# Table rows of 96 elements instead of 94, and one output store issued from another queue

## The chip, the cores and the metric

The kernel runs on one core of a Trainium2 chip. The metric is device time in microseconds of one execution, as the median of several runs; lower is better. A profile of one more execution shows each engine: TensorE (PE, with its weight loads as PEld), VectorE (DVE), ScalarE (ACT), GpSimd (POOL) and SyncE (SP), which here only issues DMAs.

## What is computed

A global filter along the sequence, then a feed-forward block with an exact GELU:

```python
X = np.fft.rfft(x, axis=1)                     # x: 8 x 3008 x 256
y = np.fft.irfft(X * (filt_r + 1j * filt_i), n=3008, axis=1)
h = y.reshape(24064, 256) @ w_in               # w_in: 256 x 2048
out = (0.5 * h * (1 + erf(h / sqrt(2)))) @ w_out   # w_out: 2048 x 256
```

Inputs and the output are float32.

## The kernel before

The sequence of 3008 is split as 47 x 64, and the Fourier transform and its inverse are each two stages of small matrix products with tables of sines and cosines. Per batch `b` the stages are `s1` (transform over 47), `s2` (over 64, then the product with the filter on VectorE), `s3` (inverse over 64) and `s4` (inverse over 47), with round trips through DRAM (`R1`, `R2`; written and read back by SP) to turn the data between them. Batch 0 has stages of its own (`c1` to `c4`), since nothing else runs beside them.

`s4` is the stage that the change touches. For each of 8 groups `grp` of positions and 2 halves of the channels it issues 4 matmuls (L513), each with 96 x 128 weights out of `d_sb` and, as the moving operand, one row of the table `T4a`: 94 columns, row number `4 * grp + i`. So there are 7 batches x 8 x 2 x 4 = 448 of them, in 112 groups of four; a group fills one PSUM bank, which ScalarE or VectorE copies (L329, L333) into the ring `y_sb`. Batch 0's `c4` (L611) has the same shape of matmul, with one table `T4c` of 96 x 94 for all its positions.

`T4a` is 96 partitions x 32 rows x 94 elements in bf16, the real and imaginary parts of a row interleaved. GpSimd makes it in `table_4_all` in four calls, each with two parts; a part is two products into a scratch tile (L410) and their sum into every second element of eight rows (L412).

The feed-forward block runs in tiles `t` of 512 rows, 47 of them. `mm1` (L635, L638) is the first product and the GELU. `mm2_first` is the second product for tile 0; for the others `mm2_seven` (L707) forms it from seven quarter-size products, as in Strassen's method, of sums that VectorE makes (`sums_1` to `sums_3`; L676, L682, L689), and VectorE combines the seven in L722 to L736 into output tiles `ost`. Each output tile of 512 rows is stored in pieces of 128 rows by `put_rows` (L754), in the order h = 1 then h = 0, and sub = 0 then 1 in each; a piece that crosses a group of 376 rows becomes two DMAs. Tiles 0 and 1 are stored by SP and the later ones by GpSimd.

The order of everything is written out by hand. The main loop at the end of the kernel goes through slots, 16 for a tile: in each slot first come the pieces that a table `at` has put there (stages of the filter for the batch ahead, loads, table work), then a share of `mm2_seven` of the tile before and then `mm1`. Each engine and each DMA queue works through its own instructions in that order. `load_next` puts a tiny copy on GpSimd (`gate`, L149) that waits for VectorE, ahead of loads of the next batch (L98), so that these don't start early. The output buffers `ost` and `t_sb` come from one pool of four.

DMAs of a kind (hardware: issued by SP or ACT; software: issued by GpSimd) take eight completion counters in turn, and a DMA waits for the one that had its counter before it.

Of the kernel before, what the change touches and what calls it, by code (L numbers as in the profile page):

```python
# [12 lines left out]
BF16 = mybir.dt.bfloat16  # L13
# [5 lines left out]
NA, NB = 47, 64  # L19
K1 = 24  # L20
HB = 32
# [10 lines left out]
class _Mix:  # L32
    def __init__(self, ctx, tc, x, filt_r, filt_i, w_in, w_out, out):
        self.tc, self.nc = tc, tc.nc
        self.x, self.filt_r, self.filt_i = x, filt_r, filt_i
        self.w_in, self.w_out, self.out = w_in, w_out, out
        self.B, self.S, self.D = x.shape
        self.DFF = w_in.shape[1]
        assert self.S == NA * NB and self.D == 256 and self.DFF == 2048
        pool = lambda name, bufs, **kw: ctx.enter_context(tc.tile_pool(name=name, bufs=bufs, **kw))  # L40
        P = bass.MemoryType.PSUM
        self.const = pool("const", 1)
        self.px = pool("px", 1)
        self.pa = pool("pa", 3)
        self.pb = pool("pb", 3)
        self.pp = pool("pp", 3)
        self.pv = pool("pv", 2)
        self.pd = pool("pd", 3)
        self.pool = pool
        self.po = pool("po", 4)  # L50
        self.py = pool("py", 1)
        self.pg = pool("pg", 2)
        self.pq = pool("pq", 1)
        self.small = pool("small", 1)
        self.dram = pool("dram", 2, space=bass.MemoryType.DRAM)
        c = self.const
        self.T1 = c.tile([2 * NA, 96], BF16, name="T1")
        self.T2p = c.tile([128, K1, 2, 2, 16], BF16, name="T2p")
        self.xs = c.tile([128, 4, 256], BF16, name="xs")
        self.U = c.tile([128, 2, 2, HB], BF16, name="U")  # L60
        self.T4a = c.tile([96, HB, 2 * NA], BF16, name="T4a")
        self.T4c = c.tile([96, NA, 2], BF16, name="T4c")
        self.F = c.tile([128, 2, K1, 256], BF16, name="F")
        self.w_in_sb = c.tile([128, 2, self.DFF], BF16, name="w_in_sb")
        self.w_out_sb = c.tile([128, 16, self.D], FP16, name="w_out_sb")
        self.w_sums = c.tile([128, 4, 8, 128], FP16, name="w_sums")
        self.ps, self.st = {}, {}
        self.flip = 0
# [333 lines left out]
    def table_4_all(self, parts):  # L402

        tt = self.nc.gpsimd.tensor_tensor
        tmp = self.pd.tile([96, 1024], FP32, tag="d", name="tmp_sb")
        a, b = (tmp[:, o:o + 8 * NA].rearrange("p (w m) -> p w m", w=8) for o in (0, 512))
        to = self.T4a.rearrange("p w (m h) -> p h w m", h=2)
        for w, h in parts:
            for o, x in ((a, 0), (b, 1)):
                tt(out=o, in0=self.fcs[:, w:w + 8, h, x:x + 1].to_broadcast([96, 8, NA]),  # L410
                   in1=self.G[:, x].unsqueeze(1).to_broadcast([96, 8, NA]), op=ALU.mult)
            tt(out=to[:, h, w:w + 8], in0=a, in1=b, op=ALU.add)  # L412
# [94 lines left out]
    def s4(self, b, grp, half, eng):  # L507
        nc = self.nc
        o = b % 2 * self.S
        d = self.st[b, "d", grp // 2]  # L510
        ps = self.bank("ps_s4")
        for i in range(4):
            nc.tensor.matmul(ps[:, 94 * i:94 * i + 94],  # L513
                             lhsT=d[:, (grp % 2) * 4 + i, 128 * half:128 * half + 128],
                             rhs=self.T4a[:, 4 * grp + i], start=True, stop=True)
        if b == self.B - 1:
            yv = self.ring[:, half, o:o + self.S].rearrange("c (m w) -> c m w", w=HB)[:, :, 4 * grp:4 * grp + 4]
        else:
            o += GRP * grp
            yv = self.ring[:, half, o:o + GRP].rearrange("c (m w) -> c m w", w=4)  # L520
        pv = ps[:, 0:376].rearrange("c (i m) -> c m i", i=4)
        self._evac(yv, pv, eng, 1.0 / self.S)
# [168 lines left out]
    def mm2_seven(self, t, lo, hi):  # L691

        nc, v = self.nc, self.nc.vector.tensor_tensor
        a11, a12, s2, a22 = self.quarters(t)
        w = self.w_out_sb.rearrange("p (i k) (n o) -> p k n i o", k=2, n=2)
        q = self.w_sums
        s31, s4 = self.st["s", t], self.st.get(("s4", t))
        ops = ((a11, w[:, 0, 0]), (a12, w[:, 1, 0]), (s2, q[:, 1]), (s31[:, :, 0], q[:, 2]),
               (s31[:, :, 1], q[:, 0]), (a22, q[:, 3]), (s4, w[:, 1, 1]))
        last = t == self.B * self.S // TCH - 1  # L700
        for n in range(lo, hi):
            m, sub, i = n // 16, n // 8 % 2, n % 8
            if n % 16 == 0 and (m == 0 or m % 2 == 1) or last and m > 4 and i == 0:
                self.st["o"] = self.bank("ps_o", "h" if n > 80 else "o").rearrange("p (m s o) -> p m s o", m=2, s=2)
            ps = self.st["o"]
            a, b = ops[m]
            nc.tensor.matmul(ps[:, (m + 1) % 2, sub, :], lhsT=a[:, i, 128 * sub:128 * sub + 128], rhs=b[:, i],  # L707
                             start=i == 0, stop=i == 7)
            if last and m > 4 and i == 7:
                self.finish(t, m, sub, ps)  # L710
            if n % 16 != 15 or m % 2 or last and m > 4:
                continue
            p0, p1 = ps[:, 0], ps[:, 1]
            if m == 0:
                self.st["t"] = self.po.tile([128, 2, 2, 128], FP32, tag="ost", name="t_sb")
                self.st["c"] = [None, None]
            if m in (2, 4):
                self.st["c"][m // 4] = self.po.tile([128, 2, 256], FP32, tag="ost", name="ost")
            t1, t3 = self.st["t"][:, 0], self.st["t"][:, 1]
            c = lambda h, k: self.st["c"][h][:, :, 128 * k:128 * k + 128]  # L720
            if m == 0:
                nc.vector.tensor_copy(out=t1, in_=p1)  # L722
            elif m == 2:
                v(out=c(0, 0), in0=t1, in1=p0, op=ALU.add)  # L724
                if last:
                    self.store(t, 0, 0, nc.sync)
                v(out=t1, in0=t1, in1=p1, op=ALU.add)
            elif m == 4:
                v(out=t3, in0=t1, in1=p0, op=ALU.subtract)  # L729
                v(out=c(1, 1), in0=t3, in1=p1, op=ALU.add)  # L730
                if last:
                    self.store(t, 1, 1, nc.scalar)
                v(out=t1, in0=t1, in1=p1, op=ALU.add)
            else:
                for h, tt, p in ((1, t3, p0), (0, t1, p1)):
                    v(out=c(h, 1 - h), in0=tt, in1=p, op=ALU.add)  # L736
                    for sub in range(2):
                        self.put_rows(t * TCH + 256 * h + 128 * sub, self.st["c"][h][:, sub],
                                      nc.gpsimd if t > 1 else nc.sync)

    def put_rows(self, r0, tile_, eng):

# [282 lines left out]
```

## Time and profile before

| | us |
|---|---|
| runs before | 743.26, 743.35, 744.1; median 743.35 |
| span of the profiled execution, first to last instruction | 741.6 |
| TensorE busy | 731.2 |
| VectorE busy | 584.7 |
| ScalarE busy | 574.6 |
| GpSimd busy | 292.9 |
| L513, 448 matmuls: busy, mean of one | 38.1, 0.206 |
| L412, 8 sums on GpSimd: busy, mean of one | 10.7, 1.336 |
| L410, 16 products on GpSimd: busy, mean of one | 14.1, 0.902 |
| L754, 227 store issues on GpSimd: busy, mean of one | 128.8, 0.574 |

The profiled execution has its own time: between its span and the median of the runs lie 1.75 us, in which no instruction of the page runs. Matmuls are pipelined, so that the lengths of neighbours overlap; the distance from one start to the next is what a matmul costs. PE's busy share therefore says that work was there, not that the array was at its peak. DMA issues count as busy time on POOL only.

### The profile page before, as it was taken

To read this page: it belongs to the slowest core of one execution; us is meant where nothing else is said; L and a number is where in the kernel's file an instruction comes from. 1 tells how busy PE (TensorE), PEld (TensorE's weight loads), DVE (VectorE), ACT (ScalarE), POOL (GpSimd) and SP (SyncE) were. 2 spreads that over 40 slices of the span, in tenths; PEclk is the share of its full clock that TensorE was granted. 3 is DMA by queue.
4 is the path that set the end of the run, shared out by engine and by line. 5 is a ranking of instruction groups with operands and counts; after the bars stand their busy time and mean duration, and the time that the engine had idled before them with its cause. 6 is when DMAs were issued, how large, how long until landed. Compare 5 with 4: busy or idle time off the path is not lost.

```text
span 741.6 us, 20996 instructions
## 1 busy us (share of the span) xinstructions
PE 731.2 (99%) x8588; PEld 507.9 (68%) x8588; DVE 584.7 (79%) x1036; ACT 574.6 (77%) x1048; POOL 292.9 (39%) x546
## 2 busy tenths in 40 slices
PE   7999999999999999999999999999999999999997
PEld 4856665666776666666777666666677666777776
DVE  7986988889877897788976889678888887675666
ACT  6997778678877888777887778877888778777773
POOL 7995356674313452135511364115531212121121
PEclk9999999999999999999999999999999999999999
DMA  9999643646265643645626555255545443311011
GB/s 150 224 201 233 163 110 97 194 102 140 76 156 143 133 101 98 188 100 125 133 85 171 120 116 137 74 156 141 110 100 136 137 111 106 92 45 43 31 58 58
DMA packets 84051, 90.79 MB, mean 122 GB/s; under 512 B 13347, under 2 KB 63011, under 8 KB 83827
## 3 DMA queue, kind: packets, MB, share of 16 engines
q1 hardware_dynamic: 61011, 49.11, 25.8%
q0 software_dynamic: 22528, 40.15, 24.3%
q8 instruction: 67, 1.10, 0.6%
q14 instruction: 29, 0.24, 0.1%
q10 hardware_dynamic: 416, 0.20, 0.1%
HBM read 57.15 MB, written 48.23 MB: 142 GB/s over the span
## 4 chain that ended last, share of the span: by engine, by line
PE 93%; DVE 3%; ACT 2%; DMA 1%; POOL 0%; issue 0%; DVEq 0%; POOLq 0%
PE ps_h L635 42%; PE ps_o L707 39%; PE ps_s L484 3%; PE ps_s L513 3%; PE ps_s L429 2%; PE ps_s L458 2%; PE ps_o L648 1%; DMA x_sb<-in_x_dram 1%; PE ps_c L582 1%; ACT y_sb L329 1%; ACT g_sb L638 1%; DVE g_sb L682 1%; DVE s_sb L676 1%; PE ps_c L560 0%; PE ps_warm L323 0%
## 5 line engine op out<-in xcount | busy, mean ns | idle before, releaser
L638 ACT ACTIVATE g_sb<-ps_h 128x512 f16<-128x512 f32 x752 | 446.6, 602 | 146.3 <-PE ps_h L635 143.5
L635 PE MATMUL ps_h<-y_sb,w_in_sb 128*128 128x512 bf16 (+3 forms) x1600 | 445.4, 366 | 0.2 <-DVE a_sb L331 0.2
L754 POOL DMA_DIRECT2D out_dram<-ost x227 | 128.8, 574 | 389.4 <-DVE ost L736 368.6
L707 PEld LDWEIGHTS <-g_sb 128*128 128x128 f16 x2944 | 193.9, 98 | 83.6 <-issue 11.6
L707 PEld LDWEIGHTS <-s_sb 128*128 128x128 f16 x2208 | 148.0, 98 | 62.0 <-issue 11.1
L635 PEld LDWEIGHTS <-w_in_sb 128*128 128x128 bf16 x1600 | 125.1, 98 | 7.2 <-issue 1.1
L707 PE MATMUL ps_o<-w_sums,g_sb 128*128 128x128 f16 x1472 | 127.4, 219 | 1.1 <-DVE g_sb L682 0.9
L707 PE MATMUL ps_o<-w_sums,s_sb 128*128 128x128 f16 x1472 | 126.2, 219 | 0.0
L676 DVE TENSOR_TENSOR s_sb<-g_sb 128x1024 f16<-128x1024 f16 x184 | 120.5, 689 | 1.0 <-ACT g_sb L638 1.0
L707 PE MATMUL ps_o<-w_out_sb,g_sb 128*128 128x128 f16 x1472 | 118.9, 219 | 0.0
L470 DVE TENSOR_TENSOR p<-ps_s,F 128x1024 bf16<-128x1024 f32 x84 | 102.0, 1217 | 5.4 <-PE ps_s L458 4.0
L98 POOL DMA_DIRECT2D x_sb<-in_x_dram x156 | 79.0, 513 | 1.1 <-PE ps_c3t L597 0.8
L729 DVE TENSOR_TENSOR t_sb<-t_sb,ps_o 128x256 f32<-128x256 f32 x46 | 19.3, 420 | 60.2 <-PE ps_o L707 60.2
L682 DVE TENSOR_TENSOR g_sb<-s_sb,g_sb 128x1024 f16<-128x1024 f16 x92 | 65.0, 707 | 1.6
L689 DVE TENSOR_TENSOR s_sb<-g_sb 128x1024 f16<-128x1024 f16 x92 | 64.1, 696 | 0.0
L707 PE MATMUL ps_o<-w_out_sb,s_sb 128*128 128x128 f16 x736 | 63.8, 219 | 0.0
L736 DVE TENSOR_TENSOR ost<-t_sb,ps_o 128x256 f32<-128x256 f32 x90 | 33.7, 416 | 20.5 <-PE ps_o L707 20.5
L513 PEld LDWEIGHTS <-d_sb 96*128 96x128 bf16 x448 | 31.9, 98 | 25.3
L329 ACT ACTIVATE y_sb<-ps_s 128x376 bf16<-128x376 f32 x94 | 46.7, 497 | 3.2 <-PE ps_s L513 3.2
L329 ACT ACTIVATE v_sb<-ps_s 128x512 bf16<-128x512 f32 x83 | 45.0, 597 | 0.2
L331 DVE CAST a_sb<-ps_s 128x512 bf16<-128x512 f32 x54 | 34.7, 684 | 12.7 <-PE ps_s L429 12.4
L724 DVE TENSOR_TENSOR ost<-t_sb,ps_o 128x256 f32<-128x256 f32 x46 | 19.1, 415 | 26.1 <-PE ps_o L707 26.1
(155 smaller groups left out, 526.8 us busy)
## 6 DMA issues: line engine op xcount, KB each, us to landing
out_dram<-ost POOLq DMA_DIRECT2D x125, 128.0 KB, 2.3
b_sb<-R SPq DMA_DIRECT2D x28, 384.0 KB, 3.9
R<-v_sb SPq DMA_DIRECT2D x84, 128.0 KB, 2.4
d_sb<-R SPq DMA_DIRECT2D x56, 192.0 KB, 3.4
R<-a_sb SPq DMA_DIRECT2D x108, 96.0 KB, 2.2
x_sb<-in_x_dram POOLq DMA_DIRECT2D x48, 94.0 KB, 2.6
x_sb<-in_x_dram POOLq DMA_DIRECT2D x48, 48.0 KB, 2.7
x_sb<-in_x_dram POOLq DMA_DIRECT2D x12, 188.0 KB, 5.4
```

The costliest lines, as they stand in the source:

```text
L98: self.nc.gpsimd.dma_start(out=xt[64 * v + to:64 * v + to + m, h, 4 * c:4 * c + 4 * n, :], in_=xv[h][at:at + m, w:w + 4 * n, :])
L329: self.nc.scalar.activation(out=out, in_=in_, func=AF.Copy, scale=1.0 if scale is None else scale)
L331: self.nc.vector.tensor_copy(out=out, in_=in_)
L470: self.nc.vector.tensor_tensor(out=self.st[b, "w"][:, :, d:4:2, :], in0=ps.unsqueeze(1).to_broadcast([128, 2, 2, 256]), in1=self.F[:, :, k ...
L513: nc.tensor.matmul(ps[:, 94 * i:94 * i + 94], lhsT=d[:, (grp % 2) * 4 + i, 128 * half:128 * half + 128], rhs=self.T4a[:, 4 * grp + i], sta ...
L635: nc.tensor.matmul(ps[:, o:o + n], lhsT=w[:, dc], rhs=self.ring[:, dc, off:off + n], start=(dc == 0), stop=(dc == 1))
L638: nc.scalar.activation(out=self.st["g", t][:, jc, :], in_=ps, func=AF.Gelu)
L676: self.nc.vector.tensor_tensor(out=self.st["s", t][:, i:i + 2], in0=a, in1=b, op=ALU.subtract)
L682: self.nc.vector.tensor_tensor(out=a21[:, k], in0=self.st["s", t][:, k, 0], in1=a22[:, k], op=ALU.add)
L689: self.nc.vector.tensor_tensor(out=self.st["s4", t][:, k], in0=a12[:, k], in1=s2[:, k], op=ALU.subtract)
L707: nc.tensor.matmul(ps[:, (m + 1) % 2, sub, :], lhsT=a[:, i, 128 * sub:128 * sub + 128], rhs=b[:, i], start=i == 0, stop=i == 7)
L754: eng.dma_start(out=out, in_=tile_[lo - r0:lo - r0 + n])
```

## The change

The row of `T4a` is declared with 96 elements, of which the first 94 are written and read; everything allocated after it in SBUF begins 128 bytes later. One store of tile 1 (h = 1, sub = 0; the first of its five DMAs) is issued by GpSimd instead of SP. The instructions of TensorE, VectorE and ScalarE and their order are the same; GpSimd's list has the store as one more entry, between loads of batch 2 for p = 4 and the gate for p = 6, and SP's has it as one less.

```diff
-        self.T4a = c.tile([96, HB, 2 * NA], BF16, name="T4a")
+        self.T4a = c.tile([96, HB, 96], BF16, name="T4a")
...
-        to = self.T4a.rearrange("p w (m h) -> p h w m", h=2)
+        to = self.T4a[:, :, 0:2 * NA].rearrange("p w (m h) -> p h w m", h=2)
...
-                             rhs=self.T4a[:, 4 * grp + i], start=True, stop=True)
+                             rhs=self.T4a[:, 4 * grp + i, 0:2 * NA], start=True, stop=True)
...
                         self.put_rows(t * TCH + 256 * h + 128 * sub, self.st["c"][h][:, sub],
-                                      nc.gpsimd if t > 1 else nc.sync)
+                                      nc.gpsimd if t > 1 or h > sub else nc.sync)
```

## The prediction

> **What bounds the kernel now.** I read the busy shares and the chain of waits first, then the windows, then the order of single instructions in the stage that the change touches.
>
> ```profile
> span 741.6 us, 20996 instructions
> PE 731.2 (99%) x8588; PEld 507.9 (68%) x8588; DVE 584.7 (79%) x1036; ACT 574.6 (77%) x1048; POOL 292.9 (39%) x546
> PE 93%; DVE 3%; ACT 2%; DMA 1%; POOL 0%; issue 0%; DVEq 0%; POOLq 0%
> ...
> 108.00:132.00 24.00, 22.88 (x257) 14.40 (x255) 20.79 (x34) 17.96 (x36) 15.92 (x20) 1.00 0.39 104
> 132.00:200.00 68.00, 68.00 (x817) 47.23 (x815) 57.73 (x97) 53.23 (x98) 36.65 (x63) 1.00 0.53 127
> 200.00:560.00 360.00, 360.00 (x4304) 250.11 (x4302) 290.03 (x504) 286.20 (x527) 131.64 (x254) 1.00 0.51 124
> ```
>
> TensorE (PE) is busy for 731.2 of 741.6 us and carries 93% of the chain. In the windows (columns: length; busy time of PE, PEld, DVE, ACT, POOL; granted clock; DMA share; GB/s) it never rests from 132 to 560 us, at clock 1.00. So a nanosecond off one matmul there is a nanosecond off the end, and a DMA or a POOL operation counts only where TensorE ends up waiting for it. The one place after the start-up where it waits is 108 to 132 us: 24.00 - 22.88 = 1.12 us idle.
>
> **The padded rows, read by TensorE.** L513 is the only reader of T4a: 448 matmuls of 94 columns, in 112 groups of four, each group between other matmuls. The same shape with the same kind of weights (96x128 of d_sb) exists once more: L611, the first batch's last stage, whose moving operand T4c always begins at the tile's start. From the timelines of PE (start, length, what):
>
> ```profile
> 313.20 0.59 PE L635 MATMUL ps_h<-y_sb,w_in_sb 128*128 128x512 bf16 x2
> 313.63 0.34 PE L513 MATMUL ps_s<-T4a,d_sb 96*128 96x94 bf16 x4
> 313.81 0.55 PE L707 MATMUL ps_o<-w_sums,s_sb 128*128 128x128 f16 x7
> ...
> 33.03 0.61 PE L597 MATMUL ps_c3t<-eye,vt_sb 128*128 128x128 bf16 x8
> 33.48 0.50 PE L611 MATMUL ps_c<-T4c,d_sb 96*128 96x94 bf16 x8
> 33.82 0.61 PE L597 MATMUL ps_c3t<-eye,vt_sb 128*128 128x128 bf16 x8
> ```
>
> Lengths overlap, so starts are what to compare. Four L513 hold the array from 313.63 to 313.81, 0.18 us; eight L611 from 33.48 to 33.82, 0.34 us, or 0.17 us for four. The rounding hides the rest, so I took the start times of the single matmuls in the trace. In L513 the four gaps to the next start have means of 45.9, 44.2, 44.4 and 44.3 ns, 178.8 ns a group. In L611 the first gap after another kind of matmul is 45 or 46 ns, and those after it 40 to 42, mean 41.3: 45.8 + 3 x 41.3 = 169.7 ns for four. The first matmul of a group costs the same in both; the second to fourth cost about 3 ns more in L513. What differs is where the moving row begins. Rows of 94 bf16 are 188 bytes; the tile begins at a multiple of 64, so row w = 4u + i begins at 0, 12, 8 or 4 bytes past a multiple of 16 for i = 0, 1, 2, 3. The one aligned row of each group is the one without the surcharge. Padded to 192 bytes, all rows begin at a multiple of 64. **Gain: 112 x (178.8 - 169.7) ns = 1.02 us**, one group less (the first, at 109.87, lies beside a wait for VectorE): 111 x 9.1 = 1.01 us.
>
> Bounds: nothing, if the surcharge has another cause (another pool of PSUM banks, neighbours that load VectorE and ScalarE); and, if the switch's 46 ns falls to 41.3 too and L707's first gap after a group (57 to 59 ns against 56 in its own run) loses 2 ns, 112 x (178.8 + 2 - 4 x 41.3) = 1.75 us. I take 1.0: it is what the nearest row shows.
>
> [...]
>
> **The padded rows, written by GpSimd.** L412 writes eight times, in 376 elements; the output becomes eight runs of 47 instead of one of 376 with the same step of 2. Rows of before: 980 ns where VectorE left it alone (149.66), about 1,320 or more where they met. L410 on the same engine, with inputs read in eight runs of 47, takes 817: so between 0.8 and, with no nearer row for a broken write, twice 980 ns. I take 980. It hardly lies on the path: T4a's second quarter, made in slot 80, is ready at 118.9 us and is first wanted by the third pair of s4 groups, near slot 110. What can reach the path is that GpSimd holds up VectorE:
>
> ```profile
> 128.57 1.61 POOL L410 TENSOR_TENSOR tmp_sb<-t_sb 96x376 f32<-96x376 f32 x2
> 130.26 1.32 POOL L412 TENSOR_TENSOR T4a<-tmp_sb 96x376 bf16<-96x376 f32 x1
> ...
> 128.18 2.56 DVE L682 TENSOR_TENSOR g_sb<-s_sb,g_sb 128x1024 f16<-128x1024 f16 x1
> ...
> 130.80 0.51 PE L707 MATMUL ps_o<-w_sums,g_sb 128*128 128x128 f16 x6 [0.72 <-DVE g_sb L682]
> ```
>
> This L682 takes 2.56 us where L682's median is 0.69, it ends 0.56 us after the second L410 (130.18), and TensorE stands still for 0.72 us. The order of POOL against DVE there is set by stores that wait for DVE, so both move together and I count 0. The bounds are one such stop gone (-0.72 us) or one more (+0.72 us).
>
> **All later tiles lie 128 bytes further on.** 32 rows x 4 bytes. Starts stay multiples of what they were (64, or 32 for the small ones), so I take 0; no row prices it.
>
> **The store that moves.** Of tile t = 1 only, h = 1, sub = 0: one issue, 128 KB. On SP:
>
> ```profile
> 80.26 3.56 SPq L754 DMA_DIRECT2D out_dram<-ost  x5
> 86.61 13.90 SPq L497 DMA_DIRECT2D R<-v_sb  x8
> ...
> 78.16 1.00 POOL L98 DMA_DIRECT2D x_sb<-in_x_dram  x2
> 83.69 0.18 POOL L149 COPY gate<-p 1x1 bf16<-1x1 bf16 x1 [4.54 <-DVE p L470]
> ```
>
> SP issues five stores from 80.26 to 83.82 and then has nothing until a v_sb of ScalarE is ready at 86.61: taking one away (3.56 / 5 = 0.71 us) shortens an idle queue, gain 0. POOL receives it between loads that end at 79.16 and a gate that waits for VectorE until 83.69. Its own wait is for L736, done at 80.24; then 0.57 us of issue (the L754 row's 574 ns mean), over by 80.9. Behind it stand that gate and four loads of the next batch, and they have 2.8 us to spare. Without that cover the loads would be 0.57 us later; batch 2's first fold, which reads the tile they fill, starts at 98.43. The buffer is wanted back by L730 of t = 2 at 90.77; POOL's stores of 128 KB land in 2.3 us (median), SP's in 2.6. Cost 0. Completion counters are dealt out in turn, so they rename by one from there on; each DMA still waits for the eighth before it of its kind, and TensorE's instructions wait for the same loads. ScalarE gains one extra wait and VectorE loses one, some 50 ns each at about 117 us: 0.
>
> [...]
>
> **Sum.** 741.6 - 1.0 + 0 + 0 = 740.6 us of span. Between the span and the runs' median of 743.35 lie 1.75 us, which the change does not touch: **742.3 us**, 0.14% less. A difference under 0.2% (1.5 us) is about what a measurement of this kernel can tell from no change.
>
> **Rivals.**
> - *The gain is larger* (0.20): the surcharge goes from all four matmuls of a group (1.75 us), or the 1.0 us comes with one stop of VectorE less (0.72): 741.6. For it: the 1.75 is the row bound, and POOL's place against DVE was unlucky. Against: L611 shows the 46 ns at a switch even with an aligned row.
> - *The surcharge is no matter of alignment* (0.25): then nothing else is left and the time is 743.35. [...] Against: the aligned first matmul is free of it. This is also the case in which the change doesn't do what it may be for.
> - *Slower* (0.13): the broken write takes L412 to twice 980 ns, so that in each of the two blocks of table work in 111 to 134 us VectorE meets GpSimd once more, as L682 did. Two stops of 0.72 and half the alignment gain or none: 743.35 + 1.44 = 744.8. It decides from about 2.5 us of added VectorE time in that window. For it: VectorE carries the chain there (115.5 to 130.8). Against: L410 reads broken runs at 817 ns.
> - *Forecast* (0.42): 742.3, its own range 742.0 to 742.7.
>
> **How the numbers follow.** Faster by over 0.2% (below 741.9): the larger gain and some of the forecast's edge where a stop goes as well, 0.20 + 0.10 = 0.30. Slower by over 0.2% (above 744.8): the slower case passes that line about half the time, and a stop with no alignment gain adds some, and the price of 128 bytes has no row: 0.14. The rest, 0.56, is within 0.2%. The range goes from 741.2, the 1.75 us with part of a stop, to 743.9, no gain and most of one stop more.
>
> **What would show it.** In the changed profile: L513's four starts 46, 41, 41, 41 ns apart (now 46, 44, 44, 44); from 132 to 655 us the same work ends about 1 us earlier; L412 still near 980 ns where undisturbed; L682 near 128 us long or short, with PE's idle time before L707 beside it; a store on POOL near 80.3 us and the gate still at 83.7. The prediction is wrong if L513's gaps stay at 44 ns, or if the difference lies before 132 us.

## The result, and the profile after

| | before | after |
|---|---|---|
| median of 11 runs, us | 743.68 | 742.41 |
| lowest and highest, us | 743.26, 744.45 | 741.84, 742.69 |
| span of the profiled execution, us | 741.6 | 740.3 |

The ratio of the runs is 0.9977, with a 95% interval of 0.9968 to 0.9986: 1.0 to 2.4 us less, 1.7 us as the middle. By 2% that counts as the same; it is just over the 0.2% that the prediction set as the limit of what can be told (the side to which it gave 0.30), and the interval lies on both sides of that limit.

The head of the page after (span; busy time, share of the span and number of records of each engine; shares of the chain):

```profile
span 740.3 us, 20857 instructions
PE 722.4 (98%) x8448; PEld 507.2 (69%) x8588; DVE 584.6 (79%) x1036; ACT 574.7 (78%) x1048; POOL 293.4 (40%) x547
PE 86%; ACT 6%; DVE 3%; issue 2%; DMA 2%; POOL 1%; DVEq 0%; POOLq 0%
```

PE seems to have lost 8.8 us of work and 7 points of the chain. It has not: 8448 matmuls are recorded where there were 8588, so 140 records are missing; that the chain's share went to other engines for the same reason is likely, but not shown. The weight loads (PEld) are complete, 8588 in both, so I compared the two executions by them: the time of each weight load after, less that of the same one before.

| up to, us | 25 | 132 | 200 | 400 | 655 | 735 | end of span |
|---|---|---|---|---|---|---|---|
| after less before, us | +0.32 | +0.32 | +0.18 | -0.11 | -0.59 | -0.59 | -1.29 |

Three things are to be seen. In the first 25 us the changed kernel loses 0.3 us, where nothing was changed; the other profiles below show that this stretch differs from execution to execution. From 132 to 655 us, where L513 runs, it earns 0.91 us, little by little. Nothing more comes up to the last weight load; then 0.69 us come at once, after the last matmul. The prediction has no such term, although the profile before showed the place. This is its last window, with the columns as in the prediction:

```profile
655.00:742.00 87.00, 82.29 (x941) 60.22 (x939) 51.62 (x107) 55.53 (x94) 14.12 (x27) 1.00 0.14 47
```

The span ends at 741.6 us, so TensorE is idle for 4.3 us of this window; the prediction's "one place after the start-up where it waits" leaves out the end.

The instructions that touch `T4a` in the profile after (duration in ns, least, median and most; first and last start in us), and one group of L513 in the timeline of PE:

```profile
L513 PE MATMUL ps_s<-T4a,d_sb x448: 202/204/208, 110.2 to 649.5; 96*128 96x94 bf16 x150
L412 POOL TENSOR_TENSOR T4a<-tmp_sb x8: 979/1326/1914, 59.3 to 150.0; 96x376 bf16<-96x376 f32 x8
```

```profile
313.24 0.59 PE L635 MATMUL ps_h<-y_sb,w_in_sb 128*128 128x512 bf16 x2
313.67 0.33 PE L513 MATMUL ps_s<-T4a,d_sb 96*128 96x94 bf16 x4
313.84 0.33 PE L707 MATMUL ps_o<-w_sums,s_sb 128*128 128x128 f16 x3
```

Four L513 now hold the array from 313.67 to 313.84, 0.17 us. Their single starts are 45.8, 40.9, 40.8 and 40.9 ns apart (before 45.9, 44.2, 44.4, 44.3). L412's shortest is 979 ns (before 980), its median 1326 (before 1324): the broken rows cost GpSimd nothing that shows. VectorE's long L682 and the matmuls that wait for it, and then the timelines of POOL and of SP around the moved store:

```profile
128.49 2.56 DVE L682 TENSOR_TENSOR g_sb<-s_sb,g_sb 128x1024 f16<-128x1024 f16 x1
...
131.11 0.51 PE L707 MATMUL ps_o<-w_sums,g_sb 128*128 128x128 f16 x6 [0.73 <-DVE g_sb L682]
```

```profile
80.83 0.60 POOL L754 DMA_DIRECT2D out_dram<-ost  x1 [1.37 <-DVE ost L736]
84.00 0.18 POOL L149 COPY gate<-p 1x1 bf16<-1x1 bf16 x1 [2.57 <-DVE p L470]
```

```profile
80.56 2.93 SPq L754 DMA_DIRECT2D out_dram<-ost  x4
86.91 2.43 SPq L497 DMA_DIRECT2D R<-v_sb  x4
```

The stop of VectorE and TensorE near 130 us is where it was, 0.73 us. GpSimd issues the store in 0.60 us and is idle for 2.57 us behind it; SP issues four and is idle afterwards. All this is as forecast, at times 0.3 to 0.5 us later, of which the start makes 0.3.

The end is not. SP's last issue in its timeline, and, from the list of SP's waits, those for stores at the kernel's end (L1020; us in total, times, longest); the first two are of the kernel before, the other two of the changed one:

```profile
737.79 0.41 SPq L772 DMA_DIRECT2D out_dram<-ost  x1
```

```profile
SPq L1020 <- DMA out_dram<-ost: 1.3, 1, 1.3
```

```profile
737.20 0.41 SPq L772 DMA_DIRECT2D out_dram<-ost  x1
```

```profile
SPq L1020 <- DMA out_dram<-ost: 0.6, 2, 0.5
```

From the start of that last issue to the end of the span it is 3.83 us before and 3.13 us after. The trace's records of SP's waits say why. In the traces of before and after, the DMAs of SP and ACT (313 and 312) update eight counters strictly in turn, those of GpSimd (417 and 418) eight others; of the 600 pairs of neighbours on one counter for which all landings are on record, in each of the two, none has the later DMA issued before the earlier one has landed. At the end SP waits for the eight counters of the hardware DMAs one after the other, in both in the order 0 to 7. Times in us from the last issue to the end of each wait:

```
counter           0     1     2     3     4     5     6     7   end of span   last store has
before         1.83  1.89  1.95  2.04  2.12  2.19  2.55  2.63     3.83        counter 0
after          0.52  0.58  0.65  0.74  0.81  1.31  1.52  1.88     3.13        counter 7
```

With 313 hardware DMAs the last store has counter 0, the first in the row: SP waits 1.83 us for it to land and then goes through seven counters that were all done before it, 0.80 us. With 312 the last store has counter 7: the others are gone through while it flies. From the last counter on it is 1.20 and 1.25 us.

Not all of the 0.70 us belongs to the counters. By the last update of its counter the store itself lands 1.81 us after its issue before the change and 1.68 us after it, 0.13 us sooner. From the landing to the end it is 2.02 and 1.45 us: 0.57 us is what the counters are worth. (SP is through with counter 7 only 0.20 us after the landing; the reason comes with five_stores.)

### The profile page after: what moved, and what is told of

The parts are those of the page before. It is cut to its first block, busy times and chain, and to the rows that moved or that the text cites. A ratio compares the mean times of both kernels' runs of the same rounds, so it can differ in the third digit from the quotient of the medians.

```text
span 740.3 us, 20857 instructions
## 1 busy us (share of the span) xinstructions
PE 722.4 (98%) x8448; PEld 507.2 (69%) x8588; DVE 584.6 (79%) x1036; ACT 574.7 (78%) x1048; POOL 293.4 (40%) x547
## 4 chain that ended last, share of the span: by engine, by line
PE 86%; ACT 6%; DVE 3%; issue 2%; DMA 2%; POOL 1%; DVEq 0%; POOLq 0%
PE ps_o L707 38%; PE ps_h L635 36%; ACT g_sb L638 3%; PE ps_s L484 3%; PE ps_s L513 3%; PE ps_s L429 2%; PE ps_s L458 2%; ACT y_sb L329 1%; ACT v_sb L329 1%; PE ps_o L648 1%; DMA x_sb<-in_x_dram 1%; DMA F<-in_filt_i_dram 1%; DVE g_sb L682 1%; PE ps_c L582 1%; DVE s_sb L676 1%
## 5 line engine op out<-in xcount | busy, mean ns | idle before, releaser
L635 PE MATMUL ps_h<-y_sb,w_in_sb 128*128 128x512 bf16 (+3 forms) x1464 | 416.2, 365 | 0.8 <-DVE a_sb L331 0.2
L707 PEld LDWEIGHTS <-g_sb 128*128 128x128 f16 x2944 | 193.9, 98 | 83.6 <-issue 11.6
L707 PEld LDWEIGHTS <-s_sb 128*128 128x128 f16 x2208 | 147.9, 98 | 62.0 <-issue 11.1
L707 PE MATMUL ps_o<-w_sums,g_sb 128*128 128x128 f16 x1472 | 127.5, 219 | 1.8 <-DVE g_sb L682 0.9
L707 PE MATMUL ps_o<-w_sums,s_sb 128*128 128x128 f16 x1472 | 126.2, 219 | 1.7
L707 PE MATMUL ps_o<-w_out_sb,g_sb 128*128 128x128 f16 x1472 | 118.9, 219 | 1.8
L682 DVE TENSOR_TENSOR g_sb<-s_sb,g_sb 128x1024 f16<-128x1024 f16 x92 | 65.0, 708 | 1.6
L707 PE MATMUL ps_o<-w_out_sb,s_sb 128*128 128x128 f16 x736 | 63.9, 219 | 0.3
L513 PEld LDWEIGHTS <-d_sb 96*128 96x128 bf16 x448 | 31.3, 97 | 25.3
```

What stands on the lines that cost most here:

```text
L513: nc.tensor.matmul(ps[:, 94 * i:94 * i + 94], lhsT=d[:, (grp % 2) * 4 + i, 128 * half:128 * half + 128], rhs=self.T4a[:, 4 * grp + i, 0:2 ...
L635: nc.tensor.matmul(ps[:, o:o + n], lhsT=w[:, dc], rhs=self.ring[:, dc, off:off + n], start=(dc == 0), stop=(dc == 1))
L682: self.nc.vector.tensor_tensor(out=a21[:, k], in0=self.st["s", t][:, k, 0], in1=a22[:, k], op=ALU.add)
```

## The experiments

All times below are medians, beside runs of the kernel before on the same chip (744.07 us for the first four, 744.05 for the next four, 743.91 for rows98, order_0213 and tab108, 743.94 for tab74). Two more columns come from the profiles: what the stretch of L513 earned against the kernel before (position of the weight loads, 132 to 655 us), and the time from the last store's issue to the end. Between 132 and 655 us rows100 (at 416 us) and tab74 and w_out_off4 (at 224 us) contain one further step of 0.14 us each, which nothing in their edits explains. Both columns are steadier than the spans: up to 80 us the profiles of kernels that do the same there lie between 0.5 us less and 2.2 us more than the kernel before.

| kernel | median, us | ratio to before, 95% | 132 to 655 us | last issue to end |
|---|---|---|---|---|
| pad_only | 743.18 | 0.9988 (0.9979 to 0.9997) | -0.91 | 3.72 |
| store_only | 743.91 | 0.9996 (0.9987 to 1.0005) | 0.00 | 3.25 |
| act_store | 744.85 | 1.0009 (1.0000 to 1.0018) | 0.00 | 3.89 |
| five_stores | 743.38 | 0.9991 (0.9982 to 1.0000) | +0.04 | 2.97 |
| rows104 | 743.16, one run | | -0.92 | 3.14 |
| rows100 | 742.64, one run | | -0.77 | 3.15 |
| rows96_off4 | 742.14, one run | | -0.89 | 3.14 |
| w_out_off4 | 742.76 | 0.9982 (0.9972 to 0.9992) | -0.77 | 3.25 |
| rows98 | 743.73, one run | | -0.62 | 3.23 |
| order_0213 | 742.50 | 0.9979 (0.9970 to 0.9989) | -0.83 | 3.21 |
| tab108 | 742.56 | 0.9979 (0.9970 to 0.9988) | -0.91 | 3.29 |
| tab74 | 742.40 | 0.9980 (0.9971 to 0.9989) | -0.76 | 3.29 |

### The two parts alone

pad_only is the changed kernel with the store back on SP; store_only is the kernel before with this one line:

```diff
-                                      nc.gpsimd if t > 1 else nc.sync)
+                                      nc.gpsimd if t > 1 or h > sub else nc.sync)
```

> The padded rows alone; all stores stay where they were (313 hardware transfers, the last store on the counter that SP waits for first at the end). Theory (two separate gains: rows 0.9 to 1.0 us, end of the kernel 0.7 us): L513's starts 46, 41, 41, 41 ns apart, as in the changed kernel; the span from the issue of the last store to the end 3.8 us, as before; 0.9 to 1.0 us below the kernel before. Rival (the whole gain belongs to the rows): 1.3 us or more below, and 3.1 us from the last issue to the end.

> The moved store alone, rows of 94 elements (312 hardware transfers, the last store on the counter that SP waits for last). Theory: L513's second to fourth starts stay 44 ns apart; the stretch from the issue of the last store to the end falls from 3.8 to 3.1 us, because seven waits of SP are gone through while the store lands and not behind it; 0.7 us below the kernel before. Rival (the store is hidden, cost 0 as predicted): no difference, 3.8 us at the end.

L513 in the profiles of pad_only and of store_only:

```profile
L513 PE MATMUL ps_s<-T4a,d_sb x448: 202/204/208, 110.1 to 649.4; 96*128 96x94 bf16 x150
```

```profile
L513 PE MATMUL ps_s<-T4a,d_sb x448: 205/205/208, 110.9 to 651.1; 96*128 96x94 bf16 x150
```

The rows alone shorten L513 and earn 0.91 us in its stretch, as much as the changed kernel earns there; by the runs 0.9 us (0.2 to 1.6). The end is 3.72 us, only 0.11 us less than before, and that is the landing, at 1.70 us. The store alone leaves L513 as it was and shortens the end to 3.25 us, which is 0.57 us less, with the landing at 1.81 us as before. The 0.70 us of the changed kernel are the two together. The time of store_only, 0.3 us less with an interval from 1.0 less to 0.4 more, agrees with this and with nothing at all; that the store brings something rests on the ends in the traces.

### Is it the queue, or the number of transfers?

```diff
-                                      nc.gpsimd if t > 1 else nc.sync)
+                                      nc.gpsimd if t > 1 else nc.scalar if h > sub else nc.sync)
```

> The same store leaves SP, but for ScalarE's queue, so that it stays a hardware transfer (313 in all, last store on the first counter). Rows of 94. Theory (the number of hardware transfers decides, not what SP is relieved of): 3.8 us from the last issue to the end, time as before within 0.2 us. Rival (SP's queue is relieved, or its transfers are): the same gain as in the kernel with the moved store alone, 0.7 us.

The end is 3.89 us: taking the store from SP doesn't help as long as it remains a hardware DMA and the last store keeps counter 0. I had not counted what ScalarE pays. ACT in the profile of act_store:

```profile
78.87 0.60 ACT L638 ACTIVATE g_sb<-ps_h 128x512 f16<-128x512 f32 x1 [0.23 <-PE ps_h L635]
80.82 0.67 ACTq L754 DMA_DIRECT2D out_dram<-ost  x1
81.54 2.70 ACT L638 ACTIVATE g_sb<-ps_h 128x512 f16<-128x512 f32 x5 [2.08 <-PE ps_o L707]
```

ScalarE stands still for 2.08 us, until the store's data are there and the issue is done; five GELUs pile up behind it, PE waits 0.50 us at 82.19, and from 80 to 90 us all work falls back by 0.66 us. The runs show 0.7 us more (0.0 to 1.3). So the forecast of "no change" missed for a reason beside the question; the end answers the question.

### All of tile 1's stores on GpSimd

```diff
-                                      nc.gpsimd if t > 1 else nc.sync)
+                                      nc.gpsimd if t > 0 else nc.sync)
```

> All of the second chunk's stores by GpSimd: 308 hardware transfers, last store on the fourth counter in SP's row of waits, so four counters are left to go through once it has landed, not seven or none. Rows of 94. Theory: 0.07 to 0.1 us for each counter, so the stretch from the last issue to the end is about 3.8 - 3 x 0.1 = 3.5 us, and the time 0.3 us below the kernel before. Rival (each transfer less saves something of its own): five times what one saves, 3 us or more. Rival (GpSimd's queue pays): slower than the kernel before.

The last store has counter 3, as meant, and the waits end as the theory has it, four left over after it, 0.24 us:

```
counter           0     1     2     3     4     5     6     7   end of span
five_stores    0.69  1.39  1.63  1.83  1.89  1.95  2.01  2.07     2.97
```

But the end is 2.97 us, shorter than after the change, where 3.5 was expected. Two pauses are gone that the theory didn't have. In 13 of the 14 profiles SP is idle for 0.33 to 0.35 us ahead of its 464th record, whichever counter that is: before the change it is the wait for counter 6 (2.19 to 2.55 above), after it that for counter 7. SP of five_stores has 463 records. And GpSimd is idle for 0.32 to 0.35 us ahead of its 709th record, in the last 1.3 us of those 13; in five_stores that record comes at 734 us, before a long wait, and no such gap is there. So one of the seven waits in the "0.80 us" is a pause of 0.29 us more, and a wait alone takes 0.06 to 0.09 us. In the changed kernel SP's pause runs from 1.55 to 1.88 us, over the landing at 1.68: that is the 0.20 us between landing and counter 7.

### What in a row costs?

All four start from the changed kernel. The first edit is rows104 (rows100 has 100 in its place); the second, with the same shift in the writing of the table, is rows96_off4, rows of 96 with the data in columns 2 to 95; the third, w_out_off4, shifts another operand:

```diff
-        self.T4a = c.tile([96, HB, 96], BF16, name="T4a")
+        self.T4a = c.tile([96, HB, 104], BF16, name="T4a")
...
-                             rhs=self.T4a[:, 4 * grp + i, 0:2 * NA], start=True, stop=True)
+                             rhs=self.T4a[:, 4 * grp + i, 2:2 * NA + 2], start=True, stop=True)
...
-        self.w_out_sb = c.tile([128, 16, self.D], FP16, name="w_out_sb")
+        w_out = c.tile([128, 16 * self.D + 32], FP16, name="w_out_sb")
+        self.w_out_sb = w_out[:, 2:16 * self.D + 2].rearrange("p (j o) -> p j o", o=self.D)
```

> The changed kernel with rows of 104 elements, 208 bytes: rows begin at multiples of 16 bytes, every second one not at a multiple of 32. Theory (what costs is a row that does not begin at a multiple of 16 bytes): L513's starts 46, 41, 41, 41 ns apart, as with rows of 96. Rival (the boundary is 32 or 64 bytes): one or more of the second to fourth gaps at 44 ns.

> The changed kernel with rows of 100 elements, 200 bytes: rows i = 0 and 2 of a group begin at a multiple of 16 bytes, rows 1 and 3 at 8 past one. Theory (multiples of 16 bytes): gaps after the four matmuls 46, 44, 41, 44 ns, 5 to 7 ns a group more than with rows of 96. Rival (multiples of 8 bytes are enough): 46, 41, 41, 41. Rival (lines of 16 bytes counted: 188 bytes from 8 past a line touch 13 lines, not 12): the same as the theory here; the kernel with all rows 4 bytes past tells those two apart.

> The changed kernel with rows of 96 elements whose data begin 4 bytes into the row: all rows begin 4 bytes past a multiple of 64, and 188 bytes from there touch 12 lines of 16 bytes, as many as an aligned row. Theory (the start decides): second to fourth gaps 44 ns, as before the change, and the first, if the surcharge adds to what a switch costs, about 49 ns (if the switch hides it, 46). Rival (the count of lines decides): 46, 41, 41, 41.

> The changed kernel with the last layer's matrix (w_out_sb, 256 bytes for each part) 4 bytes further on, so that it is read from 4 past a multiple of 16: the moving operand of 3 of 7 L707 matmuls, some 2,200 of 128 columns, on the path throughout. Theory: the surcharge is not special to L513; at 2.7 ns each as in L513 it is 6 us, if it grows with the columns (128/94) 8 us: slower than the changed kernel by 6 to 8 us. Rival (only rows of different phase after each other, or rows of 94, pay): no difference.

Means of the four gaps of a group (start to next start, ns; the start times of the trace), with those of the two runs that followed. Which bytes two rows share is counted from the sizes of the tiles in the kernel; no trace has the addresses.

| kernel | after 1st | 2nd | 3rd | 4th | rows that share 16 bytes with the row read just before |
|---|---|---|---|---|---|
| before (94, 188 bytes) | 45.9 | 44.2 | 44.4 | 44.3 | 2nd, 3rd, 4th |
| after (96, 192 bytes) | 45.8 | 40.9 | 40.8 | 40.9 | none |
| rows104 (208 bytes) | 45.8 | 40.8 | 40.7 | 40.9 | none |
| rows100 (200 bytes) | 45.9 | 40.8 | 40.8 | 40.8 | none |
| rows96_off4 (192, from 4 on) | 45.8 | 40.8 | 40.8 | 40.8 | none |
| rows98 (196 bytes) | 45.8 | 40.8 | 40.8 | 45.2 | 4th |
| order_0213 (94, in the order 0, 2, 1, 3) | 45.9 | 40.8 | 43.5 | 40.8 | 3rd |

My theory fell here. In rows96_off4 every row begins 4 bytes past a multiple of 16, and none pays; in w_out_off4 some 2,200 matmuls of L707 read from 4 bytes past, their gaps are 56.2 ns (56.0 and 56.1 in the changed kernel) where 2.7 ns more were forecast, and 6 to 8 us more were expected where the runs show the time of the changed kernel. So a start at 4 or 8 bytes past a multiple of 16 (rows100 has 8) is not what costs. A count of the lines of 16 bytes that a row touches, the rival of rows96_off4, doesn't fit either: the second and fourth rows of rows100 touch 13 of them and take 40.8 ns, the fourth of the kernel before touches 12 and takes 44.3.

What was left is the neighbour. With 188 bytes a row ends in the same 16 bytes in which the next begins (byte 187 and byte 188, and so on), and the next is the very next matmul. Two runs put that to the test.

> The changed kernel with rows of 98 elements, 196 bytes. The theory of aligned starts has fallen (rows of 100 and rows 4 bytes past showed 41 ns throughout). New theory: a matmul pays 3 to 4 ns where its row begins within the 16 bytes in which the row of the matmul just before it ended. With 196 bytes that holds for i = 3 alone (row 2 ends at byte 579 and row 3 begins at 588, both in 576 to 591): gaps after the four matmuls 46, 41, 41, 44 ns, in all groups. Rival (only rows that follow each other without a gap pay): 46, 41, 41, 41. Rival (shared 32 or 64 bytes, which rows of 100 speak against): more than one gap at 44.

> Rows of 94 elements as in the kernel before, the moved store as in the changed one, and the four matmuls of a group issued in the order 0, 2, 1, 3, each still with its own row and its own part of the PSUM tile: no row then begins where the row of the matmul before it ended. Theory (the neighbour in time decides): gaps 46, 41, 41, 41 without any padding, and the time of the changed kernel, 1.4 to 1.7 us below the kernel before. Rival (something in the rows themselves, their place or what was written there): 46, 44, 44, 44, and the time of the kernel with the moved store alone, 0.3 to 0.7 us below.

rows98 changes the 96 to 98; order_0213 keeps rows of 94 and has the moved store:

```diff
-        for i in range(4):
+        for i in (0, 2, 1, 3):
```

rows98 came out as forecast: 4.4 ns on the fourth matmul alone, the only one that shares 16 bytes (bytes 579 and 588 lie in different eights, as do 375 and 376 in the kernel before, so a shared 8 is not needed; rows100 shares 32 bytes between its second and third row and pays nothing, so a shared 32 is not enough). order_0213 frees the second and the fourth without any padding. Its third still pays 2.7 ns, which I had not forecast: row 1, read after row 2, ends in the 16 bytes in which row 2 had begun. So it seems enough that two matmuls one after the other touch the same 16 bytes, at whichever end; for that order there is only this one kernel.

How much of this is shown? That the neighbour in time decides is: in order_0213 the rows that begin 8 and 4 bytes past a multiple of 16 lie where they lay before the change, and lose their surcharge by the order alone. That the measure is a shared 16 bytes is less sure. In rows98 and in order_0213 the one row that pays is also the only one that begins 12 bytes past a multiple of 16 (588 and 188), and no kernel has such a row without a neighbour in its 16 bytes. A second surcharge for that start by itself, beside one for rows that follow each other without a gap, would give the same gaps; starts at 4 and 8 past are free of it (rows96_off4, rows100, rows98), 12 past was not tested alone.

By the runs order_0213 is 1.6 us faster than before (0.8 to 2.2), as much as the changed kernel.

### The stop at 130 us

These two kernels try to be faster than the changed one by taking GpSimd's table work away from the long L682. Both start from the changed kernel. First, in tab108, the third and fourth part come later, as printed; in tab74 the second and third come earlier, slots 15, 74, 80 and 112:

```diff
-    for i, slot in enumerate((15, 80, 96, 112)):
+    for i, slot in enumerate((15, 80, 108, 124)):
```

> The changed kernel with the third and fourth part of the table's products (L410, L412) at slots 108 and 124, not 96 and 112, so that GpSimd doesn't work beside the L682 that takes 2.56 us near 128.5 us. Theory (that L682 is long because GpSimd works beside it): L682 back to about 0.7 us, TensorE's 0.73 us of idle time at 130.4 gone, and 0.7 us less than the changed kernel, 2.3 us below the kernel before (ratio 0.997). Rival (the long operation only moves to the next place where the two meet, and TensorE waits there): the time of the changed kernel, 1.6 us below.

> The changed kernel with the second and third part of the table's products at slots 74 and 80, not 80 and 96. Moving the third and fourth part had left the third where it was in GpSimd's queue, right behind a store that waits for VectorE at 126 to 128 us. Here the second part falls into 102 to 109 us, where GpSimd waits and VectorE has 1.8 us to spare, the third to 112 us, and nothing to 126 us. Theory: the L682 near 128 us back to 0.69 us, TensorE's 0.72 us of idle time before L707 gone, 0.7 us less than the changed kernel, 2.3 us below the kernel before (ratio 0.9969). Rival (VectorE loses the same time at 102 to 109 us and carries it to 130 us): TensorE still idle by 0.5 us or more between 110 and 132 us beyond the present 0.2 and 0.2, and the time of the changed kernel, 1.6 us below.

In tab108 the third part stayed behind the same store, so L682 still takes 2.57 us (130.34) and nothing changes; this run says nothing on the question. In tab74 the cover works: the longest L682 of the whole kernel is 0.69 us (least, median and most in ns):

```profile
L682 DVE TENSOR_TENSOR g_sb<-s_sb,g_sb x92: 676/686/694, 63.7 to 731.3; 128x1024 f16<-128x1024 f16 x92
```

The waits of PE between 108 and 132 us, after the change (where the third line is the one shown further up) and then in tab74:

```profile
111.39 0.51 PE L707 MATMUL ps_o<-w_sums,g_sb 128*128 128x128 f16 x6 [0.20 <-DVE g_sb L682]
118.97 1.02 PE L635 MATMUL ps_h<-y_sb,w_in_sb 128*128 128x512 bf16 x4 [0.18 <-DVE a_sb L331]
```

```profile
109.59 0.84 PE L707 MATMUL ps_o<-w_out_sb,g_sb 128*128 128x128 f16 x12 [0.38 <-DVE ost L736]
111.40 0.51 PE L707 MATMUL ps_o<-w_sums,g_sb 128*128 128x128 f16 x6 [0.20 <-DVE g_sb L682]
119.39 1.02 PE L635 MATMUL ps_h<-y_sb,w_in_sb 128*128 128x512 bf16 x4 [0.59 <-DVE a_sb L331]
```

The 0.73 us at 130 us are gone; 0.38 us at 109.6 us and 0.41 us more at 119.4 us have come. By the weight loads, against the changed kernel, tab74 loses 0.87 us up to 120 us and gains 0.90 at 131. The time is that of the changed kernel. The rival had the time right; its sign, 0.5 us more of idle time between 110 and 132 us, is met only with the wait at 109.6 us counted in (0.41 us without it). Between 102 and 109 us, where GpSimd is now busy for 6.09 us and not 0.24, VectorE is busy for 6.47 us and not 5.16: in the two places tried, VectorE loses the time where the table work stands. Neither kernel is faster than the changed one.

## Why the prediction was right, and where it was wrong

The time was right, 742.3 forecast and 742.41 measured, and so was the direction, with a size near the limit of what can be told. The difference was less right: forecast 1.05 us, measured 1.27 between the medians and 1.7 by the ratio. The median of three runs that the forecast started from was 0.33 us below that of eleven, and this made up for part of what the sum lacked: from 743.68 the same sum would have given 742.6. That the two times agree to 0.1 us is luck.

- *The padded rows, read.* Size right, cause wrong. Forecast 1.01 us; measured 0.91 by the positions of the weight loads, in the changed kernel and in pad_only, and the gaps 46, 41, 41, 41 as forecast. By gaps alone it is 10.4 ns a group, but L707's first gap after a group grew from 58.4 to 60.4 ns and gave about 2 back. From a weight load before a group to one behind it, it is 767.8 ns before and 759.5 after: 112 x 8.3 = 0.93 us. The failed step is "What differs is where the moving row begins." The one aligned row of a group is without the surcharge, but it is also the one that has no other row of `T4a` read just before it, and the trace of before could not tell the two apart. L611 couldn't either: it reads one row again and again, which begins nowhere near where it ends. Padding to 192 bytes cures both, so the forecast held; for rows of 200 bytes the theory of aligned starts forecast 44 ns twice, and 40.8 was measured.
- *The padded rows, written:* 0, as forecast; L412 979 ns, L682 2.56 us.
- *The tiles 128 bytes further on*, counted as 0: perhaps 0.13 us, at the end. The last store lands after 1.68 to 1.70 us in all seven profiles in which `T4a` and `w_out_sb` together take 128, 384 or 640 bytes of a partition more than before, and after 1.81 or 1.82 us in the seven in which they take 0, 192 or 256 more. Whether the place of the tiles is the cause, no run tested.
- *The stop at 130 us*, priced at 0.72 us in the bounds and in a rival: mis-sized. Taken away in tab74, it returned nothing.
- *The moved store, in its place:* hidden, as forecast, by the idle time around it on POOL (2.57 us behind it) and SP (four stores issued by 83.49 us, the next DMA at 86.91). The two waits counted at some 50 ns each are shorter: the one that ScalarE gains takes 17 ns, the one that VectorE loses took 21.
- *The moved store, its counters.* This step failed: "Completion counters are dealt out in turn, so they rename by one from there on; each DMA still waits for the eighth before it of its kind", counted as 0. I followed the counters through the loop and not to the kernel's end, where the row of waits makes it matter which one is last. The three profiles with the last store on counter 0 end 3.72 to 3.89 us after its issue, the ten with it on counter 7 3.13 to 3.29; from its landing it is 2.02 to 2.07 against 1.40 to 1.60 us, 0.57 between the means and in the pair before and after.
- *1.75 us between span and time:* 742.11 - 740.3 = 1.8 in the profiled execution after.

Rows 0.91, counters 0.57 and the sooner landing 0.13 make 1.6 us, within the interval of 1.0 to 2.4. The profiled pair shows 1.29, because its start cost the changed kernel 0.3.

## What to carry to other kernels

When a surcharge follows one property of the data, list what else the cheap case has that the dear one lacks, such as its neighbour in time, before a cause is put down. Follow a change to the last instruction: whatever renumbers or counts something (a DMA more or less) may decide how the kernel ends, where nothing hides it (0.57 us here). The stall that ended on a busy engine was no gain in waiting here (0.73 us taken away in tab74, and the time stayed); ask where that engine would lose the time instead.

## What the runs showed of the hardware

- Two matmuls one after the other whose moving rows touch the same 16 bytes: the second takes 43.5 to 45.2 ns instead of 40.8, at 94 columns (before 44.2 to 44.4, order_0213 43.5, rows98 45.2); whether a row that begins 12 bytes past a multiple of 16 pays by itself stays open. A moving row that begins 4 or 8 bytes past one takes 40.8 ns (rows96_off4, rows100), against 40.8 to 40.9 in the changed kernel, where all rows begin at a multiple of 64.
- A wait of SP for a counter that is already done takes 0.06 to 0.09 us (before, after, five_stores), and waits for eight counters stand in a row at the end.
- SP pauses for 0.33 to 0.35 us ahead of its 464th record, GpSimd for 0.32 to 0.35 ahead of its 709th, in 13 of the 14 profiles, whatever these records are. In all 13 profiles that have GpSimd's pause a packet of 8 KB of the DMA queue that the page calls "instruction" begins between 0.12 us before GpSimd's pause and 0.12 us after its end; in five_stores it comes at 734.6 us and the pause is gone. For SP's pause no such packet is near, and no run tested what the pauses are; that stays open.
